# Six more 128-row groups of the value projection as seven products of halves in tile 2, and a new order of GpSimd's and VectorE's side work

## The chip, the cores and the metric

One core of a Trainium2 chip runs the whole program. The metric is the device time of one launch in microseconds (us), as the median of several runs. Five engines work side by side, each through its own list of instructions in the order in which the program was written: TensorE (PE; its weight loads are shown apart as PEld), VectorE (DVE), ScalarE (ACT), GpSimd (POOL) and SyncE (SP). An instruction waits at the head of its engine's list until the semaphores it needs are set, and everything behind it on that engine waits with it.

## The reference

A linear-attention ("retention") layer feeds a gated feed-forward layer. What is computed, cut to what matters here:

```python
# attention: 4 batches, 8 heads, 768 steps, head size 64
for t in range(S):
    state = gamma * state + einsum('bhd,bhe->bhde', k[:, :, t], v[:, :, t])
    y[:, :, t] = scale * einsum('bhd,bhde->bhe', q[:, :, t], state)
x = y.transpose(0, 2, 1, 3).reshape(3072, 512)
# feed-forward: w_gate and w_val are 512 x 1536, w_out is 1536 x 512
gate = 1 / (1 + exp(-(x @ w_gate)))
val  = x @ w_val
out  = (gate * val) @ w_out
```

## The kernel before, in words

The sequence is cut into six blocks of 128 steps. A *tile* t is one such block of all four batches: 512 tokens, held transposed as `xT[t]` (512 model dimensions on partitions in four slices `kk`, by 512 tokens). The attention of a tile is done in two halves P = 2t and 2t+1 of two batches each. The feed-forward layer of a tile has twelve hidden groups n1 = 0..11 of 128 rows each; the gated values go to `hT[t]`.

The program is an order written out by hand: `ORDER[t]` is a list of short step names for each t, and each step issues its instructions on whichever engines it uses. A minus sign means that the step works on tile t-1, and `@n` that it works on tile n. While `ORDER[t]` runs the feed-forward of tile t, it also runs the output product of tile t-1 (X and Y) and the attention that makes `xT[t+1]`. The steps that the text speaks of:

- `u3`: gate and value projection of group 3, eight 512-column products in pairs of half-width ones (tiles 1 to 4 split each product over two halves of the array, `mm`, L291), then a sigmoid on ACT (L317) and the gated product on DVE (L321). `a`, `b` are the same for half of the tokens (L336, L337).
- `g3`: only the gate of group 3 and its sigmoid (L370).
- `v21`..`v27`: value projection of *two* groups (4 and 5: the pair g = 2) as seven products of halves, a Strassen-Winograd form. The weights of the pair are a 2x2 block matrix (two groups by two halves of the model dimensions) and so is `xT` (two halves of the model dimensions by two halves of the tokens). Each product has two 256-column steps (two half-width matmuls each). It needs sums of weight blocks, `ws` (step `A2` for pair 2: four GpSimd sums, L345 to L348), and sums of `xT` blocks, `xs` (step `x1`: four DVE sums, L356 to L359). Each product ends in part-sums: copies on ACT (L395, L399), additions on DVE (L396, L400, L404), and the gated products, two on GpSimd (L401, L405) and one on DVE (L407).
- `S0 S1 S2`, `s`, and `r0`..`r11`: the same kind of sums over the gated values, `hs`, for the output product (four DVE operations for each four groups, L438; `r` issues one of the four, `s` issues all four for 128 of the columns).
- `-X1`..`-X7`, `-Y1`..`-Y7`: the output product of the tile before, also seven products. `-X1` and `-X2` read `hT` only; `-X5`, `-X3`, `-X6` read `hs`. Results go through `p` and `ob` to the output (L480 to L498); the SP queue sends them.
- `F6`, `B7`, `E7`: attention blocks, scores on PE (L201), their masks on DVE (`st`, L208), the products with the state and the values (L217, L223), and the result scaled into `xT` (L238). `O` writes the state to `zbd` (L260, ACT). `m`, `n` scale keys on ACT (L194).
- `G3`: decay tables `maskd` and `taby` of tile 3 on GpSimd (L151, L155). `W2`: sums of output weights on GpSimd and ACT (L417 to L422).
- `L8`: three loads of q, k, v, issued from GpSimd's queue (L64). `J8`: their transposition by DMA, issued from SP's queue (L181). `H7` is a one-column GpSimd copy that makes GpSimd wait until the transposed q and k of half 7 have landed (L531), and `I0` one that makes it wait until DVE has written the last of the `hs` sums (L534).

Seven PSUM banks rotate among all products (`bank`, L161). `gs` has six buffers, `scr` two, `ob` four, `hs` and `xs` one each. In the kernel before, tiles 3, 4 and 5 use the seven-product form for five pairs each (`v0..` to `v4..`), and tiles 0, 1 and 2 use it for none: tile 2 has `u0` to `u11`.

Of the kernel before, what the change touches and what calls it, by code (L numbers as in the profile page):

```python
# [17 lines left out]
def kernel(  # L18
# [142 lines left out]
    def bank(shape, dt=F32):  # L161
        return pf.tile(shape, dt, tag="ff", name="ff", padded_shape=[128, 2 * NP, C] if dt == BF16 else None)
# [174 lines left out]
        nc.vector.tensor_tensor(hT[t][:, n1:n1 + 2, lo:lo + 256], gs, ps[1], op=ALU.mult)  # L337
# [338 lines left out]
```

## Time and profile before

| | |
|---|---|
| median of 3 runs (range) | 222.92 us (222.62 to 222.94) |
| the profiled execution's own time | 223.21 us |
| its span | 221.5 us |
| PE busy | 209.5 us (95%) |
| DVE busy | 158.4 us (72%) |
| POOL busy | 123.7 us (56%) |
| ACT busy | 116.8 us (53%) |
| granted TensorE clock | full speed in all 40 slices |

A busy figure is a share of the whole span and says little about one stage. So the views used are those that cut by time: the list of waits of one engine, the busy time in a stretch, and the timeline, which gives each instruction (or a run of equal ones, "x16") with its start in us, its length, its engine and line, what it writes and reads, and, in brackets, how long the engine was idle before it and what ended that. Matmuls overlap at their ends, so a PE step is measured from its start to the next step's start.

### The profile page before, as it was taken

What the parts mean: (1) busy time and instruction counts of PE and PEld (TensorE: products, weight loads), DVE (VectorE), ACT (ScalarE), POOL (GpSimd) and SP (SyncE); (2) the same over time, 40 slices, a digit from 0 to 9 for tenths busy, and PEclk for the clock granted to TensorE, in tenths of its full rate; (3) what the DMA queues carried; (4) which work ended last, traced back from release to release, by engine and by line L of the source; (5) the groups of instructions that cost most, each with busy time, mean ns of one, the idle gap of its engine ahead of it and who ended that gap; (6) DMA issues with size and microseconds to landing.
All of it is one profiled execution on the core that took longest, in us unless ns stands there. A gap on an engine that the chain in (4) does not pass through costs nothing.

```text
span 221.5 us, 6886 instructions
## 1 busy us (share of the span) xinstructions
PE 209.5 (95%) x2924; PEld 161.7 (73%) x2924; DVE 158.4 (72%) x326; ACT 116.8 (53%) x250; POOL 123.7 (56%) x141
## 2 busy tenths in 40 slices
PE   6558999999998999999999999999999999999993
PEld 6444445799997777767779877789877777866682
DVE  6764876988659596465997579898577797544861
ACT  7584375437794336445397277635345525465231
POOL 8966886769997606999400896540243331325500
PEclk9999999999999999999999999999999999999999
DMA  9999999999995999719999899930310000220014
GB/s 126 134 172 194 196 173 156 195 186 157 132 119 53 139 198 140 215 47 120 126 134 199 136 186 157 124 73 0 145 52 0 3 3 0 95 98 0 1 44 150
DMA packets 103999, 25.35 MB, mean 114 GB/s; under 512 B 93984, under 2 KB 101152, under 8 KB 103968
## 3 DMA queue, kind: packets, MB, share of 16 engines
q0 software_dynamic: 81248, 13.90, 82.4%
q1 hardware_dynamic: 22576, 10.88, 27.5%
q8 instruction: 23, 0.38, 0.7%
q10 hardware_dynamic: 144, 0.13, 0.2%
q14 instruction: 8, 0.07, 0.2%
HBM read 28.31 MB, written 6.29 MB: 156 GB/s over the span
## 4 chain that ended last, share of the span: by engine, by line
PE 86%; DVE 5%; DMA 4%; POOL 3%; issue 0%; ACT 0%; POOLq 0%; DVEq 0%
PE ff L297 52%; PE ff L293 25%; DMA vn<-in_v_dram 4%; PE ff L201 2%; PE ff L217 2%; PE ff L223 2%; DVE xT L238 2%; PE z L245 1%; DVE hs L438 1%; DVE st L208 1%; POOL vn L64 1%; POOL kn L64 1%; POOL qn L64 1%; POOL kn L72 0%; PE ff L172 0%
## 5 line engine op out<-in xcount | busy, mean ns | idle before, releaser
L297 PE MATMUL ff<-xT,wg 128*64 128x512 bf16 (+1 forms) x480 | 50.3, 337 | 0.3 <-DVE xT L238 0.2
L401 POOL TENSOR_TENSOR hT<-gs,scr 128x512 bf16<-128x512 f32 x15 | 19.4, 1293 | 35.4 <-DVE scr L400 35.4
L297 PE MATMUL ff<-xT,wv 128*64 128x256 bf16 (+1 forms) x400 | 35.6, 307 | 1.0 <-DVE st L208 1.0
L297 PEld LDWEIGHTS <-wg 128*64 128x64 bf16 x480 | 27.7, 110 | 7.3 <-issue 0.3
L297 PEld LDWEIGHTS <-wv 128*64 128x64 bf16 x440 | 26.2, 110 | 8.8 <-issue 1.2
L321 DVE TENSOR_TENSOR hT<-gs,ff 128x512 bf16<-128x512 f32 (+1 forms) x31 | 20.6, 666 | 15.0 <-ACT gs L317 6.0
L370 ACT ACTIVATE gs<-ff 128x512 f32<-128x512 f32 x30 | 17.9, 597 | 22.3 <-PE ff L297 12.9
L317 ACT ACTIVATE gs<-ff 128x512 f32<-128x512 f32 (+1 forms) x31 | 17.8, 582 | 20.6 <-PE ff L297 11.5
L293 PE MATMUL ff<-xT,wg 128*128 128x512 bf16 (+1 forms) x100 | 25.0, 371 | 1.5 <-ACT xT L236 0.9
L208 DVE TENSOR_TENSOR st<-ff,maskd 128x512 bf16<-128x512 f32 x40 | 24.8, 682 | 1.5 <-PE ff L201 1.5
L297 PEld LDWEIGHTS <-hT 128*64 128x64 bf16 x384 | 21.4, 110 | 3.8
L405 POOL TENSOR_TENSOR hT<-gs,scr 128x256 bf16<-128x256 f32 x15 | 11.3, 756 | 12.5 <-DVE scr L404 12.5
L293 PE MATMUL ff<-xT,wv 128*128 128x512 bf16 (+1 forms) x80 | 17.5, 342 | 0.0
L260 ACT CAST zbd<-za 64x512 bf16<-64x512 f32 x20 | 12.3, 616 | 8.8 <-DVE za L252 3.2
L297 PE MATMUL ff<-wo,hT 128*64 128x256 bf16 (+1 forms) x216 | 16.2, 296 | 0.0
L293 PEld LDWEIGHTS <-wg 128*128 128x128 bf16 x100 | 9.4, 98 | 9.2 <-issue 0.9
L64 POOL DMA_DIRECT2D vn<-in_v_dram x12 | 14.0, 1170 | 2.9 <-PE ff L297 1.7
L194 ACT ACTIVATE kt<-kn,tabk 128x128 bf16<-128x128 bf16 x48 | 15.2, 390 | 0.1
L64 POOL DMA_DIRECT2D kn<-in_k_dram x11 | 12.9, 1173 | 3.2 <-DMA vn<-in_v_dram 1.5
L297 PEld LDWEIGHTS <-hs 128*64 128x64 bf16 x252 | 14.0, 110 | 0.9
L293 PEld LDWEIGHTS <-wv 128*128 128x128 bf16 x90 | 8.8, 98 | 7.6 <-issue 0.2
L64 POOL DMA_DIRECT2D qn<-in_q_dram x11 | 12.7, 1158 | 1.3 <-issue 0.6
(108 smaller groups left out, 412.3 us busy)
## 6 DMA issues: line engine op xcount, KB each, us to landing
out_dram<-ob SPq DMA_DIRECT2D x22, 256.0 KB, 2.6
vn<-in_v_dram POOLq DMA_DIRECT2D x12, 256.0 KB, 12.1
kn<-in_k_dram POOLq DMA_DIRECT2D x11, 256.0 KB, 8.5
qn<-in_q_dram POOLq DMA_DIRECT2D x11, 256.0 KB, 11.8
wo<-in_moe_w_out_dram POOLq DMA_DIRECT2D x4, 384.0 KB, 13.0
wg<-in_moe_w_gate_dram POOLq DMA_DIRECT2D x5, 256.0 KB, 9.8
wv<-in_moe_w_val_dram POOLq DMA_DIRECT2D x5, 256.0 KB, 9.5
out_dram<-ob SPq DMA_DIRECT2D x3, 128.0 KB, 2.2
```

The costliest lines, as they stand in the source:

```text
L64: nc.gpsimd.dma_start(out=held[P], in_=src(x, P))
L194: nc.scalar.activation(to[:, :, h, :], x[:, :, h, :], AX.Copy, scale=tabk[:, P // 2, h:h + 1])
L201: nc.tensor.matmul(sc[P, c][i][:, p, :], qkT[P][half, 0, c, p, :], qkT[P][half, 1, c, p, :], start=True, stop=True)
L208: nc.vector.tensor_tensor(s, sc[P, c][i], (mask0 if P < 2 else maskd[P // 2])[:, i], op=ALU.mult)
L260: nc.scalar.copy(zbd[j][half, :, :, half], za[j][half])
L293: nc.tensor.matmul(o, left, right, skip_group_check=True, **kw)
L297: nc.tensor.matmul(o[half], left[:, half], right, skip_group_check=True, **kw)
L317: nc.scalar.activation(gated[t, n1][1], gated[t, n1][3], AX.Sigmoid)
L321: nc.vector.tensor_tensor(to, gs, val, op=ALU.mult)
L370: nc.scalar.activation(sig[n1], u, AX.Sigmoid)
L401: nc.gpsimd.tensor_tensor(hT[t][:, 2 * g], sig[2 * g], v[:, 0:2].rearrange("p two n -> p (two n)"), op=ALU.mult)
L405: nc.gpsimd.tensor_tensor(hT[t][:, 2 * g + 1, 256:], sig[2 * g + 1][:, 256:], v[:, 2], op=ALU.mult)
```

## The change

Three of the six orders change, and the helpers are made more general.

- Tile 2: `u4` to `u9` are replaced by `g4` to `g9` and by the seven products of the pairs 2, 3 and 4 (`v2.`, `v3.`, `v4.`). `x1@2` is added at the end of tile 1's order, so that the `xT` sums of tile 2 exist. `S1` of tile 2 becomes `r4` to `r7`.
- GpSimd: `A0` to `A4` stood together behind `I0`. Now `A3` stands ahead of `I0`, `A2` and `A4` behind it, and `A1` and `A0` near the end of tile 2. `G3` moves from ahead of `H5 L6 L7` in tile 1 to behind them; `G5` moves behind the first gated product of tile 3. In tile 2 `H7 L8 G4 L9` come after three weight sums rather than five.
- DVE: `-s2` in tile 1 moves ahead of `b8`.
- SP: in tile 2, `J8` and `J9` now stand ahead of the outputs of `-X4` and `-Y4`.
- Tile 3: the same steps in another order.
- `val_product` becomes `half_product(kind, ...)`, and takes the second bank at product 2 rather than at product 1. A kind "q" (the gate as seven products, with sums from step `D`) is written but no order uses it.

```diff
+    wsum = {("v", g): ws[:, g] for g in range(5)}
-    def val_weight_sums(g, eng):
+    def half_sums(kind, g, eng):
...
-    def val_product(t, g, n):
+    def half_product(kind, t, g, n):
...
         if n == 1:
-            vals[g] = (bank([128, 512]), bank([128, 512]))
+            vals[kind, g] = bank([128, 512])
...
+        if n == 2 and own:
+            vals["b", g] = bank([128, 512])
...
     ORDER = [
         "u1 u2 k0 u3 k1 u4 Z0 u5 u6 Z1 s0 u7 u8 J4 J5 k2 u9 T2 u10 f2 p11",
-        "E2 -h11 V2 k3 T3 a0 a2 F3 a4 a6 E3 O2 a8 -s1 W0 b0 O3 G2 b2 W1 m4 b4 n4 b6 W2 G3 a10 b8 -s2 H5 "
-        "L6 L7 -X1 -X2 F4 m5 b10 n5 -X5 -d2 -X3 -X6 -d3 -X7 B5 J6 O4 S0 -d6 E5 J7 O5 -X4 S1 -d7 S2",
-        "-X1 -X2 u0 u1 -I0 A0 A1 A2 A3 A4 -X5 m6 u2 -X3 -X6 n6 u3 -X7 H7 L8 G4 L9 u4 -X4 F6 u5 m7 -Y1 -Y2 "
-        "u6 -Y5 n7 u7 J8 -Y3 -Y6 S0 u8 J9 -Y7 S1 u9 -Y4 B7 O6 u10 m8 E7 O7 u11 n8 S2 x1@3",
-        "-X1 -Y1 g0 -X2 -Y2 m9 -X5 -Y5 v01 v02 v05 H9 L10 L11 G5 -X3 -X6 v03 v06 -Y3 -Y6 -X7 g1 -Y7 -X4 "
-        "F8 -Y4 v07 g2 v11 v12 v15 g3 v13 v16 g4 v04 v17 n9 B9 O8 g5 v21 v22 v25 J10 g6 v23 v26 g7 v14 "
-        "v27 v31 v32 v35 J11 r0 r1 g8 v24 v33 v36 r2 r3 g9 v41 v42 v45 v37 u10 v43 v46 v34 r4 p11 v47 r5 "
-        "E9 O9 h11 v44 r6 r7 S2 x1@4",
+        "E2 -h11 V2 k3 T3 a0 a2 F3 a4 a6 E3 O2 a8 -s1 W0 b0 O3 G2 b2 W1 m4 b4 n4 b6 W2 a10 -s2 b8 H5 L6 "
+        "L7 G3 -X1 -X2 F4 m5 b10 n5 -X5 -d2 -X3 -X6 -d3 -X7 B5 J6 O4 S0 -d6 E5 J7 O5 -X4 S1 -d7 S2 x1@2",
+        "-X1 m6 A3 -X2 u0 -X5 u1 -X3 -I0 u2 A2 -X6 u3 A4 -X7 n6 H7 L8 G4 v21 L9 F6 v22 m7 v25 g4 n7 -Y1 "
+        "-Y2 v23 v26 -Y5 g5 -Y3 -Y6 v31 S0 v32 g6 g7 v27 -Y7 J8 v24 v35 J9 -X4 -Y4 v33 v36 B7 g9 v41 v37 "
+        "g8 v42 v45 r4 u10 O6 v43 r5 v46 m8 E7 v34 v47 A1 r6 r7 u11 O7 A0 n8 v44 S2 x1@3",
+        "-X1 -Y1 -Y2 -X2 v01 m9 v02 H9 -X5 L10 -Y5 g0 -X3 L11 v05 -Y3 -X6 v03 v06 -Y6 -X7 g1 G5 -Y7 v07 "
+        "F8 -X4 g2 v11 v12 v15 g3 v13 v16 g4 -Y4 v04 n9 v17 B9 O8 J10 v21 g5 v22 v25 g6 v23 v26 v14 v31 "
+        "g7 v32 v27 v35 g8 v33 J11 r0 v41 r1 v36 v42 g9 r2 v24 r3 v37 v45 u10 v43 v34 v46 p11 r4 r5 v47 "
+        "E9 v44 r6 h11 r7 O9 S2 x1@4",
```

More of the change, by code (lines that the diff above doesn't have):

```diff
@@ L339 @@
     ws = wpool.tile([128, 5, 4, KT // 2, 128], BF16, name="ws")
-    def val_weight_sums(g, eng):
+    wsum = {("v", g): ws[:, g] for g in range(5)}
+    def half_sums(kind, g, eng):
+        if kind == "q":
+            held = ld.tile([C, 2 * H, D], BF16, tag="kqv"[g % 3], name="ws", bufs=4)
+            wsum[kind, g] = held.rearrange("p (i k two) d -> p i k (two d)", i=4, k=KT // 2)
+        w = wg if kind == "q" else wv
         lo, hi = (slice(n * 128, (n + 1) * 128) for n in (2 * g, 2 * g + 1))
-        a11, a12, a21, a22 = wv[:, :2, lo], wv[:, 2:, lo], wv[:, :2, hi], wv[:, 2:, hi]
-        s1, s2, s3, s4 = (ws[:, g, i] for i in range(4))
+        a11, a12, a21, a22 = w[:, :2, lo], w[:, 2:, lo], w[:, :2, hi], w[:, 2:, hi]
+        s1, s2, s3, s4 = (wsum[kind, g][:, i] for i in range(4))
         eng.tensor_tensor(s1, a21, a22, op=ALU.add)
@@ L370, in gate @@
         nc.scalar.activation(sig[n1], u, AX.Sigmoid)
-    def val_product(t, g, n):
+    def half_product(kind, t, g, n):
         lo, hi = (slice(i * 128, (i + 1) * 128) for i in (2 * g, 2 * g + 1))
+        full = wg if kind == "q" else wv
+        own = kind == "q" or ("q", g, t) not in vals
         if n == 1:
-            vals[g] = (bank([128, 512]), bank([128, 512]))
-        ac, b = vals[g][0], vals[g][1][:, :256]
+            vals[kind, g] = bank([128, 512])
+            if kind == "q":
+                vals[kind, g, t] = True
+                if t not in hT:
+                    hT[t] = ffn.tile([128, NFF, 512], BF16, tag="hT", name="hT", bufs=2)
+                for i in (2 * g, 2 * g + 1):
+                    sig[i] = ffn.tile([128, 512], F32, tag="gs", name="gs", bufs=6)
+        if n == 2 and own:
+            vals["b", g] = bank([128, 512])
+        ac = vals[kind, g]
         a, c = ac[:, :256], ac[:, 256:]
+        if n in (2, 5):
+            b = vals["b", g][:, :256] if own else vals["b", g][:, 256:]
         for kk in range(KT // 2):
-            s = lambda i: ws[:, g, i, kk]
-            w = lambda k0, cols: wv[:, k0 + kk, cols]
+            s = lambda i: wsum[kind, g][:, i, kk]
+            w = lambda k0, cols: full[:, k0 + kk, cols]
             x = lambda k0, c0: xT[t][:, k0 + kk, c0:c0 + 256]
@@ L390, in val_product @@
             }[n]()
-            mm(t, to, left, right, start=(kk == 0 and n in (1, 2)), stop=(kk == KT // 2 - 1))
+            mm(t, to, left, right, start=(kk == 0 and (n == 1 or n == 2 and own)), stop=(kk == KT // 2 - 1))
         if n == 5:
-            vals[g, "v"] = ffn.tile([128, 3, 256], F32, tag="scr", name="scr", bufs=2)
-            v = vals[g, "v"]
+            if kind == "q":
+                vals[kind, g, "v"] = at.tile([128, 3, 256], F32, tag="maskd", name="scr", padded_shape=[128, 4, 256])
+            else:
+                vals[kind, g, "v"] = ffn.tile([128, 3, 256], F32, tag="scr", name="scr", bufs=2)
+            v = vals[kind, g, "v"]
             nc.scalar.copy(v[:, 0:3:2], ac.rearrange("p (two n) -> p two n", two=2))
             nc.vector.tensor_tensor(v[:, 0], v[:, 0], b, op=ALU.add)
-        v = vals.get((g, "v"))
+        v = vals.get((kind, g, "v"))
         if n == 6:
@@ L400, in val_product @@
             nc.vector.tensor_tensor(v[:, 1], v[:, 1], a, op=ALU.add)
+        if n == 7:
+            nc.vector.tensor_tensor(v[:, 2], v[:, 2], a, op=ALU.add)
+        if kind == "q":
+            if n == 6:
+                nc.scalar.activation(sig[2 * g], v[:, 0:2].rearrange("p two n -> p (two n)"), AX.Sigmoid)
+            if n == 7:
+                nc.scalar.activation(sig[2 * g + 1][:, 256:], v[:, 2], AX.Sigmoid)
+            if n == 4:
+                nc.scalar.activation(sig[2 * g + 1][:, :256], a, AX.Sigmoid)
+            return
+        if n == 6:
             nc.gpsimd.tensor_tensor(hT[t][:, 2 * g], sig[2 * g], v[:, 0:2].rearrange("p two n -> p (two n)"),
@@ L403, in val_product @@
         if n == 7:
-            nc.vector.tensor_tensor(v[:, 2], v[:, 2], a, op=ALU.add)
             nc.gpsimd.tensor_tensor(hT[t][:, 2 * g + 1, 256:], sig[2 * g + 1][:, 256:], v[:, 2], op=ALU.mult)
@@ L592 @@
         "g": lambda t, n: gate(t, n),
-        "v": lambda t, n: val_product(t, n // 10, n % 10),
-        "A": lambda t, g: val_weight_sums(g, nc.gpsimd),
+        "v": lambda t, n: half_product("v", t, n // 10, n % 10),
+        "q": lambda t, n: half_product("q", t, n // 10, n % 10),
+        "A": lambda t, g: half_sums("v", g, nc.gpsimd),
+        "D": lambda t, g: half_sums("q", g, nc.gpsimd),
         "x": lambda t, _: x_sums(t),
```

## The prediction

> **What bounds the kernel now.** I read the page first, then TensorE's list of waits, the busy time by tile, and the timeline at the places that the order moves.
>
> ```profile
> PE 209.5 (95%) x2924; PEld 161.7 (73%) x2924; DVE 158.4 (72%) x326; ACT 116.8 (53%) x250; POOL 123.7 (56%) x141
> ...
> PE ff L297 <- DVE st L208: 1.0, 1, 1.0
> ...
> PE ff L297 <- DVE xT L238: 0.2, 1, 0.2
> ...
> 80.45:114.26 33.81, 33.72 (x491) 24.17 (x488) 24.61 (x50) 18.37 (x44) 22.14 (x31) 1.00 1.35 133
> 114.26:147.14 32.88, 32.88 (x554) 27.28 (x552) 25.94 (x55) 20.45 (x46) 18.84 (x20) 1.00 1.51 153
> ```
>
> The two stretches are tile 2 and tile 3, from the start of one X1 step to the start of the next; the columns are length, then busy PE, PEld, DVE, ACT, POOL. PE is idle for 0.09 us of tile 2 and never in tile 3. So PE's own work sets the time there, and a change is worth what it takes out of PE's list, less any wait that it puts in. All the waits of the list after the start-up (before 17.6 us) sum to 1.2 us, both shown: 1.0 us at 67.4 and 0.2 us at 82.0, in tile 1 and at the first u0 of tile 2.
>
> ```profile
> 64.60 1.29 DVE L337 TENSOR_TENSOR hT<-gs,ff 128x512 bf16<-128x512 f32 x2 [1.21 <-ACT gs L336]
> 65.81 1.19 DVE L438 TENSOR_TENSOR hs<-hT 128x256 bf16<-128x256 bf16 x1
> 65.81 1.03 POOL L155 TENSOR_TENSOR taby<-taby,tabz 128x512 f32<-128x512 f32 x1
> 67.64 2.48 DVE L208 TENSOR_TENSOR st<-ff,maskd 128x512 bf16<-128x512 f32 x4
> 68.38 1.06 PE L297 MATMUL ff<-xT,wv 128*64 128x256 bf16 x16 [1.00 <-DVE st L208]
> ...
> 80.68 1.28 DVE L238 TENSOR_TENSOR xT<-ff,taby 128x512 bf16<-128x512 f32 x2
> 82.01 1.05 PE L297 MATMUL ff<-xT,wg 128*64 128x512 bf16 x8
> ```
>
> The reader sees step s2 (L438) on DVE: its first sum takes 1.19 us while G3's table (L155) runs on GpSimd, and later ones 0.28. The masks behind it are late, and b10's second product waits 1.0 us for the PSUM bank that the first mask frees. From 75.03 DVE is busy without a gap until xT is whole at 81.96, and u0 starts at 82.01.
>
> **The change, part by part**
>
> *1. Matmuls of tile 2.* Before, six value projections at 0.865 us each (92.40 to 93.27 for one): 5.19. After, three pairs of seven products. In tile 3 pair 2 occupies 134.28 to 134.94, 135.84 to 136.27, 137.13 to 137.59 less v14's 0.25, and v24's 0.22: 0.66 + 0.43 + 0.21 + 0.22 = 1.52; three pairs 4.56. So -0.63. But switching between 512- and 256-column steps leaves gaps of 0.03 to 0.04 (128.91 to 129.81 is 0.90 for one gate, not 0.865): tile 2 minus tile 3 should be five pairs at 0.21, 1.05, and is 33.81 - 32.88 - 0.2 (u0's wait) = 0.73. That is 0.32 of gaps for five pairs, 0.19 for three: **-0.44**. Ends: -0.63 and -0.3 (B9's start shows 0.13 more that is no pair's).
>
> *2. Tile 1: s2 ahead of b8, G3 behind L7.* POOL then has no work between W2's last sum (ends 64.66) and H5, which waits for a DMA until 67.97. DVE: a10's product 64.60 to 65.2, s2 at four pitches of 0.2 to 66.1, b8's product to 66.7, first mask done at 67.35 instead of 68.33. b10 finds its bank at 67.40: **-0.95** on PE at that point (ends -0.8, -1.0). DVE's list behind it follows PE, since B5's masks wait for scores: 75.03 becomes 74.1.
>
> *3. GpSimd's work that comes in its place.* G3 moves past six DMA issues, L6 and L7, which do not start earlier for it: H5 ahead of them waited 1.30 us for its DMA after G3's end (66.84), to 67.97. They end at 75.5 as before; then G3 (1.22 + 1.0 us) to 77.7, and A3's four sums to 80.4 (2.63 per A, from 85.10 to 87.73). DVE's S0 needs 78.3 to 79.65 (79.21 to 80.68 less 0.95) and now meets A3. What such a meeting costs shows in step s1:
>
> ```profile
> 54.98 1.20 POOL L417 TENSOR_TENSOR wt<-wo 128x512 bf16<-128x512 bf16 x1
> 55.20 1.13 DVE L438 TENSOR_TENSOR hs<-hs,hT 128x256 bf16<-128x256 bf16 x1
> 56.15 1.20 POOL L418 TENSOR_TENSOR scr<-wo 128x512 f32<-128x512 bf16 x1
> 56.26 1.24 DVE L438 TENSOR_TENSOR hT<-hT 128x256 bf16<-128x256 bf16 x1
> 57.42 0.28 DVE L438 TENSOR_TENSOR hs<-hT,hs 128x256 bf16<-128x256 bf16 x1
> ```
>
> Each DVE sum ends 0.15 us after a GpSimd operation does, one per operation; GpSimd is only 0.04 to 0.13 us slower for it. The other DVE work (L337 at 64.60 beside L151) keeps its 0.68. With A3's operations ending near 78.36, 79.1, 79.7 and 80.4, and a 512-wide sum ending 0.28 after (L438 at 141.28 took 1.50 against L401's end at 142.50), S0 ends at 80.7 instead of 79.65. xT's last two pieces (1.25) end at 81.95, and u0 starts near 82.0, where PE could have been at 80.87. So parts 2 and 3 together: **0.0**. Ends: -1.0 (A3 done before S0, or not in its way) and +1.0, below.
>
> The Trainium skill, page "SBUF — State Buffer", section "Who interferes with whom", says that a DVE instruction with two SBUF inputs contends with a GpSimd instruction that reads SBUF, and that the one that issues second "fully blocks" until the first is through. By that rule GpSimd would be held for DVE's whole sum as well, and the sum would come out as that of the slower rival, 223.5. The first half of the rule fits the 1.13 and 1.24 us above, the second does not fit GpSimd's 1.20.
>
> *4. The rest of tile 2.* x1@2 puts four DVE sums (0.42 each) behind S2, beside A2 on GpSimd: paced at 0.65 they run from 84.8 to 87.4, so u0's gated product (L321), at 84.81 before, ends at 88.0. It frees the bank that u3 takes at 89.1 (PE: u0 to 83.7, X5 .655, u1 1.73, X3, u2, X6): cover 1.1 us, price nothing. X5 now follows u0 and needs S2's first sum, at 83.75 against 83.7 plus 0.43 for its fourth pair: nothing. Loads: H7 waits for half 7's transposes; by the 5 to 7.4 us of others it is let go at 92 to 94, so L8 (98.34 before), G4, L9 (103.98) start at 92 to 94 and end at 101.5 to 104. Pair 2's gated products (L401, L405), ready near 96, stand behind them until then. v45's `scr` and r4 need them, at 108: cover 4 us. SP's J8 and J9 go ahead of X4's and Y4's outputs; J9 is through near 111 to 113 (landing of L9's q), the outputs land 3 us later, and tile 3 wants their `ob` at 120: nothing. Added work: ACT 3 x (0.585 + 0.372) = 2.9 us, DVE -6 x 0.683 + 3 x 1.67 + 1.68 = +2.6, POOL 3 x (1.293 + 0.756) = 6.1: of tile 2's 33 us DVE is then 27, ACT 21, POOL 26; all below PE.
>
> *5. Tile 2 into tile 3.* A1 and A0 (5.3 us on POOL) meet r6, r7, S2 and x1@3. Paced as above, S2's first sum is done near 116.1, its last at 118.0, the xT sums at 118.7 to 120.3, and A0's last at 119.7. PE, at X1 by 113.8, wants them for X5 at 117.0, X3 at 119.1, v05 at 119.8, v03 at 121.3: the new order of tile 3 puts the four products that read no sums, and v01 and v02, ahead. Only Y2's fourth pair (115.5) may wait for v44's product (115.65): +0.1 at most; I take **0.05**. Tile 3 otherwise has the same PE work: 0 (ends -0.2, its gaps, and +0.3).
>
> Sum against the profiled execution: 223.21 - 0.44 + 0.0 + 0.05, with -0.05 for u0 near 81.95 instead of 82.01: 222.77. That execution is 0.29 above the median of the runs, so the forecast is 222.92 - 0.45 = **222.45 us**.
>
> **The rivals**
>
> - *A3 does not delay xT.* Then the 0.95 us of part 2 stays: 222.92 - 0.45 - 0.95 = **221.5**. For it: GpSimd's start into G3 hangs on a DMA landing and could fall earlier or later, and S0 may slip in front. Against: the four sums have only 2.7 us in which to avoid it, and S0 must run in the middle of them.
> - *A3 and S0 exclude each other fully* (the other side). If each A3 operation and each S0 sum take turns with 0.66 + 0.34 us, S0 ends at 81.7, u0 starts at 83.0 against 82.01 now, and nothing later gives it back, as tile 2 has no idle PE time: 222.92 - 0.45 + 1.0 = **223.5**. It decides from the point at which u0 starts after 82.9 (slower by 0.45 in all). For it: sums of 1.19 to 1.50 us beside GpSimd. Against: GpSimd's lengths in the s1 rows. The same turn-taking at the end of tile 2 would make S2 late for X5 by about as little as its cover, 0.9 us.
> - *The seven products save nothing* (a pair has 28 half-width weight loads against 16 for two projections, in 1.52 us instead of 1.73): 222.92 - 0.0 = **222.9**. Against: tile 3 keeps the pitch of 0.22 us per product.
>
> **How the numbers follow.** A change of 0.2% is 0.45 us, about what a measurement of this kernel tells from none, and the likeliest case lies on that bound. Chances: the sum as worked out 0.50 (half of it beyond the bound, half within, 222.1 to 222.8); A3 not in the way 0.25 (faster); exclusion, or another wait of its size among the reordered side work, 0.20 (slower); nothing saved 0.05 (within). Faster 0.50, same 0.30, slower 0.20. For 8 in 10 the range takes both outer cases: 221.3 (221.5 less tile 3's 0.2) to 223.6.
>
> **What would show it.** Tile 2 from u0 to tile 3's X1: 32.25 us before (82.01 to 114.26), 31.8 if part 1 holds, 32.25 if it does not. b10's wait on L208 gone: part 2. In DVE's timeline near 79 the four sums of S0 at 0.6 us or more beside A3, and a wait of about 1 us of u0 for xT L238: part 3; a wait under 0.3 us is the faster rival, u0 past 82.9 the slower one. No wait of PE on L321, on `scr`'s banks or on `hs` in tile 2 and 3: parts 4 and 5; a wait there of 0.5 us or more makes the forecast wrong.

## The result, and the profile after

The changed kernel is slower. Its median is 224.58 us (224.04 to 227.49) against 222.88 us (222.18 to 225.35) for the kernel before on the same chips, 19 runs each. The ratio is 1.0088 with a 95% interval of 1.0061 to 1.0115: +1.96 us (+1.36 to +2.56). The ratio leaves out one execution in a slower state and is not the quotient of the medians (1.0076). The forecast was 222.45 us, in a range of 221.3 to 223.6. So the sign was wrong, and the time lies outside the range.

The profiled execution of the changed kernel took 225.39 us with a span of 223.6 us. First its page (busy time by engine), then PE's list of waits between 60 and 160 us (engine, line, what it waited for: us in total, times, longest), then the busy time in tile 2 (first u0 to X1) and in tile 3 (X1 to X1).

```profile
PE 210.8 (94%) x2960; PEld 164.9 (74%) x2960; DVE 165.1 (74%) x336; ACT 119.6 (53%) x256; POOL 132.7 (59%) x147
```

```profile
PE ff L297 <- DVE xT L238: 1.4, 1, 1.4
PE ff L297 <- DVE scr L422: 0.9, 2, 0.7
PE ff L297 <- DVE ob L517: 0.3, 1, 0.3
PE ff L297 <- DVE scr L420: 0.3, 1, 0.3
```

```profile
82.53:115.55 33.02, 32.01 (x501) 24.96 (x502) 26.55 (x56) 18.68 (x43) 21.00 (x25) 1.00 1.60 166
115.55:149.20 33.65, 33.17 (x552) 27.15 (x549) 28.68 (x56) 20.76 (x46) 25.77 (x29) 1.00 1.07 112
```

The wait of b10 for a mask (L208) is gone. In its place stand five waits, 2.9 us in all, and every one of them is for a DVE instruction. No engine became busier than PE; DVE is at 74%. So the averages say nothing, and the places have to be looked at. (In the changed file the helpers have moved by some lines: L438 is now L468, L401 L432, L405 L435, L400 L420, L404 L422, L356 to L359 L361 to L364, L345 to L348 L350 to L353, L487 L517.)

To compare all kernels by place I use the length of four stages of PE, worked out from the timelines as the difference of the starts of two PE steps: a0 to F4's scores (tile 1), F4 to the first u0 of tile 2, that u0 to X1 (tile 2), and X1 to the next X1 (tile 3). Outside these the kernels differ in the stretch before a0 (42.55 to 45.59 us) and by at most 0.23 us behind tile 3. The names of the experiments come below.

```
us              a0-F4   F4-u0   tile 2   tile 3
before          22.57   16.50   32.25    32.70
before, again   23.17   15.31   32.24    32.70
after           22.50   16.61   33.02    33.66
after, again    22.47   16.63   33.05    33.65
e1_tables       22.51   15.31   32.25    32.70
e2_s0           22.58   15.05   32.45    33.67
e3_l9           23.77   16.17   32.14    33.67
e4_a10          22.75   16.64   32.59    33.16
e5_mended       22.62   15.06   33.12    32.72
e7_a3a4         22.46   17.13   32.24    32.70
e8_t3           22.46   15.75   32.24    33.07
e9_undo         22.50   16.62   34.11    33.07
e10_mended2     22.46   15.76   31.68    32.69
e11_writes      22.62   15.31   32.25    32.69
```

Two things stand out. Tiles 2 and 3 of the changed kernel are 0.77 and 0.96 us longer, and a second profile of each kernel repeats all four of these lengths within 0.03. F4 to u0 repeats in the changed kernel (16.61, 16.63), but not in the kernel before: three profiles of the same code up to there (before, before again, and e8_t3, which changes only tile 3) give 16.50, 15.31 and 15.75.

The starts also give what a wait costs. The list counts a wait from the modelled end of the matmul before, and matmuls overlap at their ends. By the starts each wait costs 0.16 to 0.21 us more than its figure in the list: the step ahead of v24 (Y7, from 101.48 to 103.05) takes 1.57 us, the same kind of step (X7, at 91.40) 0.65, so that v24's listed 0.74 costs 0.92. In the same way u0's 1.39 costs 1.56 (16.61 against e2_s0's 15.05), v47's 0.26 costs 0.43, X7's 0.32 costs 0.49, v44's 0.16 costs 0.35, and in the kernel before b10's 1.00 costs 1.18.

**Tile 1 into tile 2.** The timeline of the changed kernel (start, length, engine, line, operation, out <- in; in brackets the engine's idle time and what ended it):

```profile
64.91 0.28 DVE L468 TENSOR_TENSOR hs<-hT 128x256 bf16<-128x256 bf16 x1
...
66.44 2.48 DVE L208 TENSOR_TENSOR st<-ff,maskd 128x512 bf16<-128x512 f32 x4
...
78.43 0.41 DVE L468 TENSOR_TENSOR hs<-hT 128x512 bf16<-128x512 bf16 x1
78.58 0.80 POOL L351 TENSOR_TENSOR ws<-ws,wv 128x256 bf16<-128x256 bf16 x1
78.88 0.78 DVE L468 TENSOR_TENSOR hs<-hs,hT 128x512 bf16<-128x512 bf16 x1
79.34 0.85 POOL L352 TENSOR_TENSOR ws<-wv 128x256 bf16<-128x256 bf16 x1
79.58 0.89 DVE L468 TENSOR_TENSOR hT<-hT 128x512 bf16<-128x512 bf16 x1
80.15 0.84 POOL L353 TENSOR_TENSOR ws<-wv,ws 128x256 bf16<-128x256 bf16 x1
80.39 0.89 DVE L468 TENSOR_TENSOR hs<-hT,hs 128x512 bf16<-128x512 bf16 x1
81.20 1.27 DVE L238 TENSOR_TENSOR xT<-ff,taby 128x512 bf16<-128x512 f32 x2
...
82.53 1.06 PE L297 MATMUL ff<-xT,wg 128*64 128x512 bf16 x8 [1.39 <-DVE xT L238]
```

s2's first sum takes 0.28 us instead of 1.19, and the masks come early: the move of s2 and G3 does what it should. Then S0 (L468) and A3 (L351 to L353) run side by side. From the second on, each DVE sum ends 0.28 to 0.29 us after a GpSimd operation, both engines' instructions are stretched (DVE from 0.41 to 0.89, GpSimd from 0.66 to 0.85), and they advance together by one sum in 0.81 us. xT is late by that, and u0 waits 1.39 us.

**Tile 2.** Two waits. The first, in time order:

```profile
100.83 1.55 POOL L432 TENSOR_TENSOR hT<-gs,scr 128x512 bf16<-128x512 f32 x1
101.18 1.49 DVE L468 TENSOR_TENSOR hs<-hT,hs 128x512 bf16<-128x512 bf16 x1
102.59 0.41 DVE L422 TENSOR_TENSOR scr<-scr,ff 128x256 f32<-128x256 f32 x1
...
103.05 0.41 PE L297 MATMUL ff<-xs,wv 128*64 128x256 bf16 x4 [0.74 <-DVE scr L422]
```

L432 is pair 2's gated product on GpSimd, let go behind L9's loads. It meets the fourth sum of S0, which takes 1.49 us instead of 0.42; behind that sum on DVE stands the addition after v27 (L422), and v24, whose product goes into the bank that L422 reads, waits 0.74 us. The second:

```profile
111.25 1.23 ACT L260 CAST zbd<-za 64x512 bf16<-64x512 f32 x2
112.50 0.37 ACT L419 COPY scr<-ff 128x256 f32<-128x256 f32 x1
...
112.92 0.41 DVE L420 TENSOR_TENSOR scr<-scr,ff 128x256 f32<-128x256 f32 x1
...
113.39 0.41 PE L297 MATMUL ff<-xs,ws 128*64 128x256 bf16 x4 [0.26 <-DVE scr L420]
```

v46's copy on ACT (L419) stands behind O6's casts (L260), so the addition (L420) is late and v47 waits 0.26 us.

**Tile 3.**

```profile
119.26 0.85 POOL L350 TENSOR_TENSOR ws<-wv 128x256 bf16<-128x256 bf16 x1
119.50 0.89 DVE L468 TENSOR_TENSOR hs<-hT,hs 128x512 bf16<-128x512 bf16 x1
120.31 0.88 DVE L361 TENSOR_TENSOR xs<-xT 128x512 bf16<-128x512 bf16 x1
...
124.19 0.41 DVE L517 TENSOR_TENSOR ob<-p,ff 128x256 f32<-128x256 f32 x1
...
124.65 0.84 PE L297 MATMUL ff<-wt,hT 128*64 128x256 bf16 x12 [0.32 <-DVE ob L517]
```

A1 and A0 (L350 to L353, from 116 to 122.5 us) run beside S2 and x1@3: seven of their eight sums take 0.71 to 0.89 us where the kernel before has 0.42 (L438 and L356 to L359). The last `xs` sum ends at 123.27, DVE's outputs come behind it, and X7 waits 0.32 us for one. A last wait, 0.16 us of v44 at 149.00, is taken up with e8_t3.

### The profile page after: what moved, and what is told of

Same layout as the page of the kernel before. It is cut to its first block, busy times and chain, and to the rows that moved or that the text cites. A ratio compares the mean times of both kernels' runs of the same rounds, so it can differ in the third digit from the quotient of the medians.

```text
span 223.6 us, 6976 instructions
## 1 busy us (share of the span) xinstructions
PE 210.8 (94%) x2960; PEld 164.9 (74%) x2960; DVE 165.1 (74%) x336; ACT 119.6 (53%) x256; POOL 132.7 (59%) x147
## 4 chain that ended last, share of the span: by engine, by line
PE 65%; DVE 15%; DMA 13%; POOL 3%; issue 2%; ACT 1%; DVEq 0%; POOLq 0%
PE ff L297 42%; PE ff L293 18%; DMA qn<-in_q_dram 6%; DVE hs L468 4%; DMA wg<-in_moe_w_gate_dram 4%; DMA vn<-in_v_dram 3%; DVE xT L238 3%; PE ff L201 2%; DVE st L208 2%; PE ff L217 1%; PE ff L223 1%; POOL kn L64 1%; DVE hT L468 1%; PE z L245 1%; DVE hT L321 1%
## 5 line engine op out<-in xcount | busy, mean ns | idle before, releaser
L432 POOL TENSOR_TENSOR hT<-gs,scr 128x512 bf16<-128x512 f32 x18 | 23.6, 1313 | 41.8 <-DVE scr L420 41.8
L375 ACT ACTIVATE gs<-ff 128x512 f32<-128x512 f32 x36 | 21.5, 597 | 28.2 <-PE ff L297 18.8
L297 PEld LDWEIGHTS <-wg 128*64 128x64 bf16 x480 | 28.2, 110 | 8.3 <-issue 1.8
L297 PE MATMUL ff<-xT,wv 128*64 128x256 bf16 (+1 forms) x376 | 32.0, 295 | 0.0
L297 PEld LDWEIGHTS <-wv 128*64 128x64 bf16 x428 | 25.4, 110 | 6.6 <-issue 1.2
L208 DVE TENSOR_TENSOR st<-ff,maskd 128x512 bf16<-128x512 f32 x40 | 24.8, 681 | 0.7 <-PE ff L201 0.7
L321 DVE TENSOR_TENSOR hT<-gs,ff 128x512 bf16<-128x512 f32 (+1 forms) x25 | 16.5, 660 | 9.8 <-PE ff L293 5.6
L435 POOL TENSOR_TENSOR hT<-gs,scr 128x256 bf16<-128x256 f32 x18 | 13.5, 750 | 16.9 <-DVE scr L422 16.8
L317 ACT ACTIVATE gs<-ff 128x512 f32<-128x512 f32 (+1 forms) x25 | 14.3, 580 | 16.3 <-PE ff L293 9.5
L260 ACT CAST zbd<-za 64x512 bf16<-64x512 f32 x20 | 12.3, 615 | 7.7 <-DVE za L252 3.2
L297 PE MATMUL ff<-xs,ws 128*64 128x256 bf16 x156 | 15.1, 273 | 0.3 <-DVE scr L420 0.3
```

The lines of the kernel that those rows point to most:

```text
L208: nc.vector.tensor_tensor(s, sc[P, c][i], (mask0 if P < 2 else maskd[P // 2])[:, i], op=ALU.mult)
L260: nc.scalar.copy(zbd[j][half, :, :, half], za[j][half])
L297: nc.tensor.matmul(o[half], left[:, half], right, skip_group_check=True, **kw)
L317: nc.scalar.activation(gated[t, n1][1], gated[t, n1][3], AX.Sigmoid)
L321: nc.vector.tensor_tensor(to, gs, val, op=ALU.mult)
```

## The experiments

Three theories were set against each other. T1: DVE sums over two SBUF operands and GpSimd's sums hold each other up, and what is queued behind the DVE sum makes PE wait, at several places. T2: the side orders (queues, the order of tile 3) make waits of their own, with no such meeting. T3: the seven products cost PE more than they save. Times are medians of the kernel and of the kernel before beside it, in us. No kernel leaves out any of the computation.

**e1_tables: the kernel before, with only s2 and G3 moved.**

```diff
- b6 W2 G3 a10 b8 -s2 H5 L6 L7 -X1
+ b6 W2 a10 -s2 b8 H5 L6 L7 G3 -X1
```

> The kernel before with one part of the change only: step s2 ahead of b8, and G3 behind L6 L7. Theory (VectorE's sums with both inputs in SBUF and GpSimd's operations that read SBUF take turns, and each wait that the change put in is such a meeting): without A3 behind it G3 is over by 77.8, before S0 starts at 78.3, so nothing collides, b10's wait of 1.0 us goes and stays gone: 0.9 to 1.0 us faster than before, ratio 0.9955 to 0.996, and u0 starts near 81.0. Rival (VectorE is simply full from 75 us on, whatever GpSimd does): the gain is lost again at u0, within 0.3 us of before.

Measured: 222.14 against 222.82, ratio 0.9971 (0.9945 to 0.9997), so -0.65 us (-1.23 to -0.07); F4 to u0 is 15.31. This part is a gain alone, and smaller than the 0.95 us that I took from one profile. Why shows in the kernel before, profiled again (timeline):

```profile
66.56 1.04 POOL L155 TENSOR_TENSOR taby<-taby,tabz 128x512 f32<-128x512 f32 x1
...
68.23 0.28 DVE L438 TENSOR_TENSOR hs<-hT 128x256 bf16<-128x256 bf16 x1
```

In this execution G3's table was through before s2 began, s2's first sum took 0.28 us, and b10 did not wait at all. PE had come late in this execution (see again_before below). But other profiles of the same tile 1, at full clock there, differ as well: in e8_t3 and e7_a3a4 that sum took 1.19 us and b10 waited 0.23 and 0.32; in e11_writes it took 0.77 and b10 did not wait. The wait that part 2 removes is there in some executions and not in others, by how the two engines stand to each other.

**e7_a3a4: the kernel before, with A3 and A4 ahead of I0.**

```diff
- -X1 -X2 u0 u1 -I0 A0 A1 A2 A3 A4 -X5
+ -X1 A3 A4 -X2 u0 u1 -I0 A0 A1 A2 -X5
```

> The kernel before with A3 and A4 taken from behind I0 and put ahead of it: GpSimd, idle from 75.5, runs A3 to 78.1 and A4 to 80.8, and S0 (79.2 to 80.7 before) meets A4 and nothing else is changed. Theory: the four sums take 0.7 to 0.9 us each, S0 ends near 81.7, and u0's wait of 0.2 us becomes 1.1 to 1.3: 0.9 to 1.1 us slower than before, ratio 1.004 to 1.005. Rival (a sum is held once, by the operation that runs when it comes): 0.3 to 0.5 us, ratio 1.0015 to 1.002.

**e11_writes: the same place, but GpSimd only writes.** A3 and six fills of A4's buffer stand ahead of I0; A4 overwrites the fills later.

```diff
+        "M": lambda t, n: [nc.gpsimd.memset(ws[:, 4], 0.0) for _ in range(n)],
...
- -X1 -X2 u0 u1 -I0 A0 A1 A2 A3 A4 -X5
+ -X1 A3 M6 -X2 u0 u1 -I0 A0 A1 A2 A4 -X5
```

> The kernel before with A3 ahead of I0 and, in the place where A4 met S0 in the run with both, six GpSimd memsets that read nothing (they fill the buffer that A4 later writes). Theory (what is shared is a way to read SBUF): S0's sums keep 0.42 us beside the memsets and the time is that of before within 0.2 us, ratio 0.999 to 1.001. Rival (any GpSimd work beside the sums slows them, the writing too): the sums take 0.7 us or more, ratio 1.003 or more.

Measured: e7_a3a4 223.62 against 222.48, ratio 1.0053 (1.0039 to 1.0067), +1.18 us; e11_writes 222.52 against 222.70, 0.9997 (0.998 to 1.0014), no difference. The timelines at S0, e7_a3a4 first:

```profile
79.41 0.85 POOL L347 TENSOR_TENSOR ws<-wv 128x256 bf16<-128x256 bf16 x1
79.65 0.89 DVE L438 TENSOR_TENSOR hT<-hT 128x512 bf16<-128x512 bf16 x1
...
82.60 0.62 PE L297 MATMUL ff<-xT,wg 128*64 128x512 bf16 x4 [1.39 <-DVE xT L238]
```

```profile
78.27 4.98 POOL L596 MEMSET ws<- 128x1024 bf16 x5
78.98 0.42 DVE L438 TENSOR_TENSOR hs<-hs,hT 128x512 bf16<-128x512 bf16 x1
...
81.32 1.05 PE L297 MATMUL ff<-xT,wg 128*64 128x512 bf16 x8
```

GpSimd is busy beside S0 in both. Where it sums `ws`, S0's sums take up to 0.89 us and u0 waits 1.39; where it only fills, they keep 0.42 and u0 does not wait. So it is not enough that GpSimd is at work, or that it writes. The runs fit that what stretches S0 is that GpSimd's instruction reads; a fill is another kind of operation too, and no run has a GpSimd sum that does not read SBUF. The Trainium skill, page "SBUF — State Buffer", section "Who interferes with whom", makes the same distinction for a GpSimd operation that reads SBUF, and the two rows agree with that.

**e2_s0: the changed kernel, with S0 behind E5**, so that xT's last pieces are made first.

```diff
- J6 O4 S0 -d6 E5 J7 O5
+ J6 O4 -d6 E5 S0 J7 O5
```

> The changed kernel with S0 of tile 1 issued behind E5 rather than ahead of it: the same work, but the four sums that meet A3 no longer stand ahead of the last two pieces of xT. Theory: u0's wait of 1.39 us falls under 0.3 us, and 1.0 to 1.2 us of the changed kernel's 1.95 us go: ratio to before 1.0035 to 1.0045. The sums still meet A3 and are still long. Rival (VectorE's total work is the limit there): the wait moves to X5, which needs S2's first sum, and the time stays within 0.4 us of the changed kernel, ratio 1.007 to 1.009.

Measured: 223.55 against 222.82, ratio 1.004 (1.001 to 1.007); F4 to u0 15.05, no wait for xT; tile 3 unchanged at 33.67. Against the changed kernel that is 0.0048 of the time, 1.07 us, for one step moved by two places. It agrees with e7_a3a4's 1.18, and nearly half of the loss is left (0.0040 of 0.0088): the meeting of S0 and A3 is not all of it. Each of the two ratios has an interval of about 0.6 us on either side, and tile 2 is 32.45 in this profile: v24's wait is gone too, since the timing shifted, and X5, which the rival spoke of, takes 0.99 us and not 0.65. So the 1.07 may hold more than the one meeting.

**e3_l9: the changed kernel, with L9 behind v26**, so that pair 2's product leaves GpSimd before S0's sums.

```diff
- v21 L9 F6 v22 m7 v25 g4 n7 -Y1 -Y2 v23 v26 -Y5
+ v21 F6 v22 m7 v25 g4 n7 -Y1 -Y2 v23 v26 L9 -Y5
```

> The changed kernel with L9 (three loads on GpSimd's queue) behind v26 rather than ahead of it, so that pair 2's gated product runs at 97.4 to 98.7 and S0 of tile 2 (100.0 to 101.6) meets load issues only. Theory: S0's fourth sum takes 0.42 us instead of 1.49, L422 is 1.0 us earlier and v27's wait of 0.74 us goes: 0.7 us faster than the changed kernel, ratio 1.005 to 1.006. Rival (v27 waits because VectorE has more work in tile 2, not because of the meeting): v27 still waits 0.4 us or more, ratio 1.007 to 1.009.

Measured: tile 2 is 32.14 instead of 33.02, S0's fourth sum 0.42 instead of 1.49, and v24 does not wait. But the time is 224.82 against 222.82, ratio 1.0098 (1.0077 to 1.012): no gain. In its profile, tile 1 holds what tile 2 gives back:

```profile
62.27 0.41 PE L297 MATMUL ff<-xT,wg 128*64 128x256 bf16 x3 [1.00 <-issue]
...
101.36 0.42 DVE L468 TENSOR_TENSOR hs<-hT,hs 128x512 bf16<-128x512 bf16 x1
```

PE stood for 1.00 us inside a gate of tile 1, where the profile shows nothing that it waited for and where no step was changed. The kernel before, profiled again, has such a gap of 0.4 us, at the same place: in both, 13 of a gate's 16 matmuls are done and F4's scores start 4.27 us later. Whether every execution of e3_l9 has it isn't shown; its six runs took 224.38 to 225.96 us, none shorter than the changed kernel's shortest, 224.04. The cause of v24's wait is shown by the lengths; its worth in the median is not.

**e4_a10: the changed kernel, with A1 and A0 earlier**, away from S2 and x1@3.

```diff
- g6 g7 v27 -Y7 J8 v24 v35 J9 -X4 -Y4 v33 v36 B7
+ g6 g7 v27 A1 -Y7 J8 v24 v35 J9 -X4 -Y4 v33 v36 A0 B7
...
- v34 v47 A1 r6 r7 u11 O7 A0 n8 v44
+ v34 v47 r6 r7 u11 O7 n8 v44
```

> The changed kernel with A1 moved behind v27 and A0 behind v36, where GpSimd stood idle for 2.5 and 3.2 us and VectorE has no sums with two inputs in SBUF; near the end of tile 2 none is left. Theory: r6, r7, S2 and the xT sums of tile 3 go back to about 0.42 us each (from 0.7 to 0.95), X7's wait of 0.32 us and Y2's goes, tile 3 is 0.5 to 0.6 us shorter: ratio 1.006. Rival (tile 3's new order itself costs the 0.96 us that it is longer): tile 3 stays within 0.2 us of 33.66 us.

Measured: 224.59 against 222.82, ratio 1.0088 (1.0061 to 1.0114), no gain in the time. By stages, tile 3 fell from 33.66 to 33.16: S2's four and x1@3's four sums are back at 0.42 and X7 doesn't wait. That is the part of A1 and A0. In tile 2 (32.59) v24 does not wait here either: GpSimd's product starts at 101.62, when S0's sums are over. But a new wait stood up (timeline):

```profile
109.44 0.66 POOL L353 TENSOR_TENSOR ws<-wv,ws 128x256 bf16<-128x256 bf16 x1
110.07 0.72 POOL L435 TENSOR_TENSOR hT<-gs,scr 128x256 bf16<-128x256 f32 x1
110.82 0.43 DVE L468 TENSOR_TENSOR hs<-hT 128x512 bf16<-128x512 bf16 x1 [0.96 <-POOL hT L435]
...
112.57 0.41 PE L297 MATMUL ff<-xs,ws 128*64 128x256 bf16 x4 [0.71 <-DVE scr L420]
```

A0 now stands ahead of a gated product (L435); r4 on DVE waits 0.96 us for that, the addition after v46 (L420) is behind r4 and r5, and v47's wait grows from 0.26 to 0.71. Moving work off one meeting put it into another queue. The stages of this profile sum to 0.65 us less than those of the changed kernel; the interval of 0.6 us on either side neither shows nor excludes that.

**e8_t3: the kernel before, with only tile 3 in the new order.**

```diff
- -X1 -Y1 g0 -X2 -Y2 m9 -X5 -Y5 v01 v02 v05 H9 L10 L11 G5 -X3
+ -X1 -Y1 -Y2 -X2 v01 m9 v02 H9 -X5 L10 -Y5 g0 -X3 L11 v05 -Y3
...
- u10 v43 v46 v34 r4 p11 v47 r5 E9 O9 h11 v44 r6 r7 S2 x1@4
+ u10 v43 v34 v46 p11 r4 r5 v47 E9 v44 r6 h11 r7 O9 S2 x1@4
```

> The kernel before with tile 3's new order alone; A0 to A4 stay behind I0. Of the 0.97 us by which tile 3 is longer in the changed kernel, the run with A1 and A0 moved left 0.46. Theory: those 0.46 us are the order's own (a sum of r that meets pair 3's or 4's gated product ahead of L422 of v47), so tile 3 takes 33.1 us here against 32.70: ratio 1.002. Rival (they come from what tile 2 hands over): tile 3 at 32.7, ratio 1.000.

Measured: 222.63 against 222.48, ratio 1.0027 (1.0009 to 1.0044); by the ratio +0.60 us (0.20 to 0.98). Tile 3 is 33.07 against 32.70. Its timeline:

```profile
144.00 1.39 POOL L401 TENSOR_TENSOR hT<-gs,scr 128x512 bf16<-128x512 f32 x1 [1.30 <-DVE scr L400]
144.30 1.38 DVE L438 TENSOR_TENSOR hs<-hs,hT 128x512 bf16<-128x512 bf16 x1
145.60 0.41 DVE L404 TENSOR_TENSOR scr<-scr,ff 128x256 f32<-128x256 f32 x1
...
146.06 0.41 PE L297 MATMUL ff<-xs,wv 128*64 128x256 bf16 x4 [0.16 <-DVE scr L404]
```

One more place of the same kind: r5 now stands ahead of v47's addition (L404) and meets the gated product (L401), 1.38 us instead of 0.42, and v44 waits 0.16. The changed kernel has the same four rows at 147 to 149 us. By the starts this one wait is all that the order costs: the step ahead of v44 takes 0.80 us (145.26 to 146.06) and 0.46 in the kernel before, and up to that step the two are within 0.03 us of each other.

**e9_undo: the changed kernel without the seven products in tile 2** (u4 to u9 back, x1@2 left out as nothing reads it, all else as the order stands).

```diff
- v21 L9 F6 v22 m7 v25 g4 n7 -Y1 -Y2 v23 v26 -Y5 g5 -Y3 -Y6 v31 S0 v32 g6 g7 v27 -Y7 J8 v24 v35 J9
- -X4 -Y4 v33 v36 B7 g9 v41 v37 g8 v42 v45 r4 u10 O6 v43 r5 v46 m8 E7 v34 v47 A1
+ u4 L9 F6 m7 u5 n7 -Y1 -Y2 -Y5 -Y3 -Y6 S0 u6 u7 -Y7 J8 J9
+ -X4 -Y4 B7 u8 u9 r4 u10 O6 r5 m8 E7 A1
```

> The changed kernel with the seven products of tile 2 undone: u4 to u9 come back for g4 to g9 and the three pairs, x1@2 goes, and every other step keeps its new place. Theory (the seven products save 0.44 us of PE and cost 0.27 us in v46's wait): tile 2 at 32.2 to 32.4 us from u0 to X1, the time within 0.3 us of the changed kernel, ratio 1.008 to 1.010. Rival (the seven products are what makes tile 2 and 3 slow): tile 2 under 32.0 us or tile 3 back at 32.7, ratio 1.005 or less.

Measured: 225.20 against 222.48, ratio 1.0117 (1.0103 to 1.0131), slower still. Tile 2 is 34.11, and two of PE's waits are the undoing's own (timeline):

```profile
98.71 0.85 PE L297 MATMUL ff<-wo,hs 128*64 128x256 bf16 x12 [0.68 <-ACT p L510]
...
105.79 0.85 PE L297 MATMUL ff<-wt,hT 128*64 128x256 bf16 x12 [0.81 <-DVE ob L520]
```

With the pairs gone, the Y steps follow one another with nothing between them, and each waits for the last one's copies. Neither of the two forecasts for tile 2 came, and as a measure of the seven products this run failed; that they cost more than they save (T3) is answered by e3_l9 (32.14) and e10_mended2 (31.68), which keep them and are below the 32.25 of six plain projections. One thing it does show. A1 and A0 keep their place in the order, but GpSimd, without the gated products, is through with them before S2 comes: S2's and x1@3's sums take 0.42 us beside load issues, X7 does not wait, and tile 3 is 33.07, as in e8_t3.

**e5_mended: four mends in one.** S0 behind E5; A1 and A0 as in e4_a10; r4 and r5 later; tile 3 in the order of the kernel before.

```diff
- J6 O4 S0 -d6 E5 J7 O5
+ J6 O4 -d6 E5 S0 J7 O5
...
- v42 v45 r4 u10 O6 v43 r5 v46 m8 E7 v34 v47 A1 r6 r7 u11 O7 A0 n8 v44 S2 x1@3
+ v42 v45 u10 O6 v43 v46 r4 m8 E7 v34 r5 v47 r6 r7 u11 O7 n8 v44 S2 x1@3
```

> The changed kernel with every meeting that the traces show taken out of the path: S0 of tile 1 behind E5; A1 behind v27 and A0 behind v36; r4 and r5 of tile 2 behind v46 and v34, so that L420 of v46 does not stand behind a sum that waits for GpSimd; and tile 3 in its order of before. Theory: u0 at its 1.4 us gain (F4 to u0 15.05 us against 16.50), tile 2 at 31.8 to 31.9 us (the matmul saving of 0.44 us without v46's wait), tile 3 at 32.7: together 1.8 us faster than before, 0.6 us faster than part 2 of the change alone, ratio 0.991 to 0.994. Rival (the seven products load the other engines of tile 2 beyond what it can hide): tile 2 at 32.2 us or more, no faster than part 2 of the change alone, ratio 0.996 to 0.998.

Measured: 222.85 against 222.48, ratio 1.0005 (0.9993 to 1.0017). The loss is gone, F4 to u0 is 15.06 and tile 3 32.72, but tile 2 is 33.12. PE's timeline in tile 2 names three waits of 0.90 us together:

```profile
82.80 0.41 PE L297 MATMUL ff<-wt,hs 128*64 128x256 bf16 x4 [0.25 <-DVE hs L468]
...
110.61 0.41 PE L297 MATMUL ff<-xs,ws 128*64 128x256 bf16 x4 [0.26 <-DVE scr L420]
...
113.14 0.41 PE L297 MATMUL ff<-xs,wv 128*64 128x256 bf16 x4 [0.39 <-DVE scr L422]
```

S0 behind xT makes S2 late for X5, which here follows u0; O6's casts are still ahead of v46's copy; and r5 ahead of v47 delays v47's addition. By the starts they cost 0.41, 0.43 and 0.60, together the 1.44 us by which this tile 2 is longer than that of the next run. The hoped-for gain did not come.

**e10_mended2: the same, with these three mended.** X5 behind u1, X3 and I0 behind u2, O6 and all of r4 to r7 behind v47. A1, A0, S0 and tile 3 are as in e5_mended.

```diff
- -X1 m6 A3 -X2 u0 -X5 u1 -X3 -I0 u2 A2 -X6
+ -X1 m6 A3 -X2 u0 u1 -X5 u2 -X3 -I0 A2 -X6
...
- v42 v45 r4 u10 O6 v43 r5 v46 m8 E7 v34 v47 A1 r6 r7 u11 O7 A0 n8 v44 S2 x1@3
+ v42 v45 u10 v43 v46 m8 E7 v34 v47 O6 r4 r5 r6 r7 u11 O7 n8 v44 S2 x1@3
```

> The second mended version: as the first (S0 of tile 1 behind E5; A1 behind v27, A0 behind v36; tile 3 in its order of before), but X5 behind u1 again, since the first left it waiting 0.7 us for S2's first sum, and in tile 2 v46 ahead of O6, with r4 to r7 behind v47, since ACT's copy for v46 stood behind O6's and L422 of v47 behind a sum. Theory (every loss is a place where one engine's list has something in front of what PE waits for, and none is the seven products' own): F4 to u0 15.05 us, tile 2 31.8 us, tile 3 32.7 us: 1.4 to 1.9 us faster than before, ratio 0.992 to 0.994, and faster than part 2 of the change alone (0.9971). Rival (tile 2's other engines cannot carry the added work): a new wait of 0.4 us or more in tile 2, ratio 0.996 or more.

Measured: 221.26 against 222.70, ratio 0.9944 (0.9922 to 0.9965): 1.25 us (0.78 to 1.74) faster than the kernel before. Its busy time in tiles 2 and 3:

```profile
80.91:112.59 31.68, 31.68 (x506) 23.86 (x502) 25.41 (x56) 19.21 (x46) 25.82 (x33) 1.00 1.69 154
112.59:145.28 32.69, 32.69 (x552) 27.07 (x549) 26.68 (x58) 20.87 (x46) 19.34 (x21) 1.00 1.27 140
```

PE is busy for all of both tiles. F4 to u0 is 15.76 and not the expected 15.05, for a wait that part 2 of the change makes possible: b8's product (L337), whose bank b10 takes, now stands behind s2 on DVE.

```profile
66.66 1.06 PE L297 MATMUL ff<-xT,wg 128*64 128x256 bf16 x16 [0.51 <-DVE hT L337]
```

The work is that of the changed kernel: the same products, sums, copies and loads. From 1.0088 to 0.9944 is 3.2 us, and it is order alone.

The two kernels were also run again beside e10_mended2 and e11_writes.

> The kernel before once more, for a second profile. The stretch from F4 to u0 was 16.50 us in its first profile, and 15.75 in the run with tile 3's order alone, whose tile 1 is the same. Theory (b10's wait depends on whether s2's first sum meets G3's table, which shifts by tenths of a us from run to run): F4 to u0 lies between 15.7 and 16.5, and the wait on L208 between 0.2 and 1.0. Rival: 16.50 again, and the other run was an exception.

> The changed kernel once more, for a second profile and times beside the mended version. Its first profile had v27 wait 0.74 us behind a sum of S0 that met GpSimd's product; the three runs with the same S0 did not. Theory (that meeting hangs on tenths of a us, the other three losses do not): F4 to u0 16.6, tile 2 32.1 to 33.0, tile 3 33.65 us; ratio 1.006 to 1.010. Rival: the meeting is there each time, tile 2 33.0.

The changed kernel gave 224.41 against 222.70, ratio 1.0085 (1.0063 to 1.0107), with the same waits in the same places. v24's wait was there again (0.77), so for that place the rival was right. The kernel before gave the second profile used above, one execution of 225.08 us. Its F4 to u0 of 15.31, without a wait, lies outside both expectations. 2.65 us of its time lie ahead of a0 (45.59 us against 42.94). They are not a late load: PE's last long wait for one, for q, ends at 11.51 us, and at 11.85 in the first profile. The page's row of the granted clock (40 slices of 5.6 us, tenths of full speed) shows about half speed in two of them, 11 to 22 us, where a step of four 512-column matmuls takes 1.33 us (from 20.84) and not 0.86:

```profile
PEclk9955999999999999999999999999999999999999
```

The four stages lie behind it.

## Why the prediction was wrong, point by point

The steps of the forecast beside the profiles:

| place | forecast | after - before, first profiles | what the runs add |
|---|---|---|---|
| F4 to u0 (parts 2 and 3) | 0.0 | +0.11 | -0.65 (e1_tables) and +1.07 to +1.18 (e2_s0, e7_a3a4): about +0.5 |
| tile 2 (parts 1 and 4) | -0.44 | +0.77 | 31.68 is possible (e10_mended2) |
| tile 3 (part 5) | +0.05 | +0.96 | 0.50 from A1 and A0 (e4_a10), 0.37 from the order (e8_t3) |

With the runs' value for the first row the three make about 2.2 us, in the interval of +1.36 to +2.56. The costs by the starts account for the third column: -1.18 (b10) - 0.27 (u0's wait before) + 1.56 (u0's now) = +0.11; -0.57 (part 1) + 0.92 + 0.43 = +0.78; and 0.49 (X7) + 0.35 (v44) + 0.11 (the first four output steps, 2.73 against e8_t3's 2.62) = +0.95. That the first row came out near the forecast's 0.0 is partly luck: the profile of before that both use is one with a long wait of b10.

*Part 1 (matmuls of tile 2, -0.44) held.* e10_mended2's tile 2 has no wait and is 0.57 us shorter than before, between the ends that I gave (-0.63 and -0.3). The -0.44 was a little small for a misread edge: X1 behind tile 3 starts at 146.96 and not at 147.14, tile 3 is 32.70 and not 32.88, so the gaps come to 0.14 us for five pairs rather than 0.32, and the term to -0.55. The rival "the seven products save nothing" is out. The mark that I had set for part 1, u0 to X1 at 31.8, was missed (33.02) because the waits lie in the same stretch.

*Part 2 (b10's wait, -0.95) held as a mechanism, and was oversized.* The wait went. But 0.95 us was read from one execution, and the kernel before has it in only some of them. e1_tables measures 0.65 us. And s2 ahead of b8 can put a wait of its own in its place (0.51 in e10_mended2's profile).

*Part 3 (A3 meets S0) held, and nearly with its size.* On the clock of the first profile (the changed kernel's F4 comes 0.41 us later, so that is taken off) S0 ended at 80.87 and u0 started at 82.12, forecast 80.7 and 82.0. The pace was 0.81 us a sum rather than the 0.65 that I took from s1, and S0 began 0.3 us earlier than I had it. The 1.0 us that I gave for full turn-taking, from which u0 would start after 82.9, did not come. That price was a sum of two pitches, and the rows do not refute the exclusion itself (last section): 0.28 us of each DVE sum and 0.53 us of each GpSimd sum follow one another, 0.81 in all. In the s1 rows a 256-wide sum ends 0.15 us after GpSimd's operation, and GpSimd hardly lost time; I carried that over to sums of 512.

*Part 4 (the rest of tile 2: nothing) failed,* by 1.0 us of listed waits, 1.35 by the starts. I had the event: pair 2's gated product stands behind L9 and runs at 101. I priced it by who needs its result (`scr`, r4, with 4 us of cover) and not by who runs beside it: S0's fourth sum, stretched from 0.42 to 1.49 us, with v27's addition behind it on DVE and v24 waiting for the bank (0.74). v47's 0.26 came from a queue that I left out, O6's casts on ACT ahead of v46's copy. PE has no wait for u0's product (L321) or for X5's sums, as I had it. My own mark, no wait on `scr`'s banks of 0.5 us or more, is the one that was broken.

*Part 5 (tile 2 into 3: 0.05) failed most.* The meeting of A1 and A0 with S2 and x1@3 was foreseen, but at one sum per 0.65 us with the last 6.5 us behind X1's start (120.3 against 113.8); at 0.81 a sum they ran until 7.7 us behind it (123.27 against 115.55). I compared the times with when PE wants the sums, and those covers held: PE's list has no wait for `hs` or `xs`. I did not follow what is queued behind the last sum on DVE: the additions and outputs (L511, L517) whose banks X7 and later steps take. And the new order of tile 3, which I took at 0 with an end of +0.3, costs 0.37 by its profile, by the same meeting once more (r5 and L401 in e8_t3). Only Y2's wait, +0.1 at most, was of the right size (0.11).

Small slips besides: the sum gives 222.48 and not 222.45, and H5's row starts at 68.15, not 67.97. Neither moves the forecast by 0.1 us.

T1 is shown at three places by runs that take away the meeting or its cause (e2_s0 and e7_a3a4 with e11_writes; e3_l9; e4_a10 and e9_undo), and e8_t3 has the fourth. By the starts these four cost 1.56 + 0.92 + 0.49 + 0.35 = 3.3 us in the changed kernel's profile. T2 is a part too, but the smaller one: v47's copy behind O6, 0.43 us, gone once O6 stands behind v47 (e10_mended2). The forecast's chance for "exclusion, or another wait of its size among the reordered side work" was 0.20. It named the right mechanism and gave too little weight to there being four such places in the new order, each able to make PE wait where tile 2 and 3 of the kernel before have no idle PE time to give it back.

What stays open: the 1.0 us gap of PE in e3_l9 and with it the worth of v24's wait in the median; how often the kernel before meets G3's table; the price of undoing the seven products alone.

## What to carry to other kernels

When a change puts reading work on GpSimd, list every two-operand SBUF sum that DVE does in the same stretch, give each its length beside GpSimd (here 0.8 to 1.5 us for 0.42), and then follow what is queued behind it on DVE until a PE bank or operand comes up: the result that the sum delivers is seldom the one that is late. Where PE has no idle time in a stage, every such place adds up, so a forecast of "covered" needs a row for each. A single profile of the kernel before can hold a wait that other executions of it don't have; look at a second one before a removed wait is counted, and take what a wait costs from the starts of the steps.
